# Zero rows, later reciprocals, a fourth step masked on VectorE, and early expert units in an attention and expert kernel

## The chip, the cores and the metric

The kernel runs on one core of one Trainium2 chip. The metric is the device time of one execution in microseconds, as the median of several runs. A profiled execution gives the trace; its span goes from the first to the last instruction.

## The reference

Three parts follow one another. All arithmetic is float32.

```python
# attention: q, k, v of (2, 8, 576, 64); each row of scores keeps its 32 largest
scores = scale * q @ k^T
kth = np.partition(scores, -32, axis=-1)[..., -32:-31]
scores = np.where(scores >= kth, scores, -1e9)
attn = exp(scores - max); attn = attn / (sum(attn) + 1e-09)
x = attn @ v                                   # put together as (1152, 512)
# experts: 4 of them, w1 (4, 512, 1024), w2 (4, 1024, 512)
p = domain_probs / (domain_probs.sum(-1) + 1e-09)
x = sum_e p[:, e] * (relu(x @ w1[e]) @ w2[e])
# gated layer: w_a, w_b (512, 1536), w_out (1536, 512), given in float64
out = ((x @ w_a) * (x @ w_b)) @ w_out
```

## The kernel before, in words

**Tokens.** The 576 positions of a batch are 4 tiles of 128 rows and a remainder of 64 rows (`REM`); the two remainders make a ninth tile, `MIX`. The nine tiles stand in four groups of 1, 2, 3 and 3 tiles. Attention goes by *steps*: for each group, for each of four pairs of heads, one step for each tile, 36 in all (steps 0 to 3, 4 to 11, 12 to 23, 24 to 35). A step has two heads, x = 0 and 1.

**One step.** TensorE makes the scores, ScalarE copies them out of PSUM (line 582), VectorE finds the 32 largest by four rounds of MAX8 (line 603) and three MATCH_REPLACE8 (609) for each head. Then a chain: GpSimd makes the two end values (649), ScalarE a steep ReLU (656), GpSimd the difference (659), ScalarE the exponential with its sum (666), GpSimd adds 1e-9 (675), VectorE takes the reciprocal (676), ScalarE scales the rows (679). TensorE transposes them (line 365), ScalarE copies the transposes out (706 for the 512 full columns, 710 for the last 64), and TensorE multiplies by v (362): for each head four products over 128 rows and one over 64 rows, the two heads side by side in 64 columns each. Step 3 (`URGENT`) ends the first group; there the difference and the addition run on VectorE. At the last tile of a pair the columns are copied out: into `xf` for the first group (738), into `xs` as a high and a low part for the others (744, 746).

**Experts and gated layer.** The first group's tile runs in float32 (`plain`): w1 and w2 are loaded as they are into places `wraw` (3) and `pw` (1) of 512 KB each, every fourth load into `pw`. The first of its eight halves of the first layer is done pair by pair, as the pairs' columns come. The other groups (`experts`) run on weights split into two float32r parts: a raw place, then ScalarE (767), then GpSimd or VectorE (768) into one of four split places. An expert's first layer needs the columns of all four pairs of its group. After all groups the gated layer runs, with its own split of the float64 weights.

**Order.** Nothing is in the order of the code. Each operation is added to a `Plan` with an engine, a duration, a key and the places it uses; `Plan.order` walks through time with these durations, takes on each engine the ready operation with the lowest key, and gives places out as they come free. The result is the order of issue on each engine, and each engine keeps it on the chip. Attention has keys by its step number, expert work 500 and 1000 upwards, evictions and weight differences negative ones, which go first. All loads go out on one queue, SyncE's.

Of the kernel before, what the change touches and what calls it, by code (L numbers as in the profile page):

```python
# [16 lines left out]
TOPK = 32  # L17
# [17 lines left out]
class Slots:  # L35


    def __init__(self, name, aps, region=None, spans=None):
        self.name, self.aps, self.region, self.spans = name, aps, region, spans
        self.free = set(range(len(aps)))  # L40
        self.queue, self.next = [], 0

# [33 lines left out]
class Plan:  # L76
# [14 lines left out]
    def order(self):  # L91
# [72 lines left out]
        while len(done) < len(self.ops):  # L164
# [32 lines left out]
            while queue and queue[0][0] <= now:  # L197
                _, _, op = heapq.heappop(queue)
                if op is None:
                    continue  # L200
                for t in op.tiles:
                    t.users -= 1
                    if not t.users:
                        t.slots.free.add(t.slot)
# [33 lines left out]
PAIRED, URGENT = (), 3  # L238


def body(tc, q, k, v, probs, w1, w2, wa, wb, wo, out):
# [42 lines left out]
    ident = const("ident", [128, 128])  # L284
    identr = const("identr", [128, 128], F32R)
    pr = const("pr", [128, NT, E])
# [5 lines left out]
    vrem = [const(f"vrem{b}", [REM, H, D]) for b in range(B)]  # L292
# [14 lines left out]
    raw = Region("raw", 3 * 1024, F32)  # L307
    wraws = raw.slots("wraw", 3, 1024)
    low = Region("low", 12800, F32)
# [27 lines left out]

    ps = psp.tile([128, 8, 512], F32, name="ps", tag="ps")
# [45 lines left out]
    def consts():  # L384
        make_identity(nc, ident)
        nc.vector.tensor_copy(identr, ident)
        nc.gpsimd.memset(qm.bitcast(F32), 0.0)
        nc.gpsimd.memset(facs[:, :, 0], -scale)
        nc.gpsimd.memset(facs[:, :, 1], STEEP)

    ready = gpsimd(1900, consts, -1e6, (), ())

    loads = []
    for i, t in enumerate(TILES):
        for rows_, view in token_rows(t, probs):
            loads.append(load(lambda i=i, rows_=rows_: pr[rows_, i], lambda view=view: view, 2.0, nbytes=4096))
# [7 lines left out]
    shared = vector(900, shares, 3.5, loads, ())  # L404
# [13 lines left out]
    def keys(b, h2, key, eng):  # L418
# [27 lines left out]
        for j in range(2):  # L446
# [8 lines left out]
            o = tensor(5 * TURN_R, turn, key + 0.02, sp[j] + krem_done[b][h + j] + [ready], [at, st_])  # L455
# [21 lines left out]
    def start_pair(c, h2, n):  # L477
# [65 lines left out]
        for b in batches(tiles):  # L543
# [5 lines left out]
            if b not in vrem_done:  # L549
                vrem_done[b] = load(lambda b=b: vrem[b], lambda b=b: last_rows(v, b), n - 2.4, (), (), 131072)  # L550
        return pair

    def scores(pair, j, i, n):
# [24 lines left out]
        o = tensor(4 * len(bs) * mm_r(HALF), emit, n - AHEAD, after, [at] + used)  # L578
# [8 lines left out]
    def masked(sd, n):  # L587

        m8, ends, sums = m8s.tile(), endss.tile(), sumss.tile()
        W = TOPK + 17 if n in PAIRED else TOPK  # L590
        m8v = lambda: m8.ap[:, 0:2 * W].rearrange("p (x n) -> p x n", x=2)
# [3 lines left out]
        last = []  # L595

        def top(x, src, c0, rounds, width, key, done):

            for r in range(rounds):
# [5 lines left out]
                )  # L605
                if r < rounds - 1:
# [9 lines left out]
        for x in range(2):  # L616
            s = sd[x][0]
            key = n + (0.4 if urgent else 0.001) * x
            if n not in PAIRED:
                last.append(top(x, [lambda s=s: s.ap, lambda x=x: e[x].ap], 0, TOPK // 8, S, key, sd[x][1]))  # L620
                continue


            got = []
            for i, op in enumerate((ALU.max, ALU.min)):
                half = lambda x=x, i=i: e[x].ap[:, i * HALF:(i + 1) * HALF]
                po = gpsimd(
                    pool_(HALF), lambda s=s, half=half, op=op: nc.gpsimd.scalar_tensor_tensor(half(), s.ap[:, 0:HALF], 1.0, s.ap[:, HALF:S], op0=ALU.mult, op1=op),
                    n - 0.4 + 0.1 * i, [sd[x][1]], [s, e[x]],
                )  # L630
                got.append(top(x, [half, half], TOPK * i, TOPK // 8 // (i + 1), HALF, key + 0.005 * i, po))

            o = vector(
                85, lambda x=x: nc.vector.tensor_tensor(
                    m8v()[:, x, TOPK:TOPK + 16], m8v()[:, x, TOPK - 2:TOPK - 18:-1], m8v()[:, x, TOPK:TOPK + 16], op=ALU.min
                ), -600, got, [m8],
            )
            last.append(vector(
                85, lambda x=x: nc.vector.tensor_reduce(
                    out=m8v()[:, x, TOPK + 16:W], in_=m8v()[:, x, TOPK - 1:TOPK + 16], axis=mybir.AxisListType.X, op=ALU.max  # L640
                ), -600, [o], [m8],
            ))

        ks = -3000 if urgent else n + 0.1
        out_, ex = [], []
        for xs_ in ([0], [1]) if urgent else ([0, 1],):
            x0, x1 = xs_[0], xs_[-1] + 1
            en = gpsimd(
                150, lambda x0=x0, x1=x1: nc.gpsimd.tensor_tensor(endv()[:, x0:x1], m8v()[:, x0:x1, ::W - 1], facs[:, x0:x1], op=ALU.mult),  # L649
                -4000 if urgent else -500, [last[x] for x in xs_] + [ready], [m8, ends],  # L650
            )
            for x in xs_:
                s = sd[x][0]

                a = scalar(
                    S, lambda x=x, s=s: nc.scalar.activation(e[x].ap, s.ap, AF.Relu, bias=endv()[:, x, 1:2], scale=-STEEP),  # L656
                    ks, [en], [s, e[x], ends], sbuf=True, ptr=True,
                )
                sub = lambda eng, x=x, s=s: eng.tensor_tensor(e[x].ap, s.ap, e[x].ap, op=ALU.subtract)  # L659
                if urgent:  # L660
                    b = vector(dve(S), lambda sub=sub: sub(nc.vector), ks, [a], [s, e[x]], port=True)
                else:
                    b = gpsimd(pool_(S), lambda sub=sub: sub(nc.gpsimd), ks, [a], [s, e[x]])
                ex.append(scalar(
                    S,
                    lambda x=x: nc.scalar.activation(  # L666
                        e[x].ap, e[x].ap, AF.Exp, bias=endv()[:, x, 0:1], scale=scale, accum_out=sums.ap[:, x:x + 1]
                    ),
                    ks, [b], [e[x], ends, sums], sbuf=True, ptr=True, extra=92,
                ))  # L670
            sv = lambda x0=x0, x1=x1: sums.ap[:, x0:x1]
            if urgent:
                sm = vector(70, lambda sv=sv: nc.vector.tensor_scalar(sv(), sv(), 1e-9, None, op0=ALU.add), ks, ex[-1:], [sums])
            else:
                sm = gpsimd(290, lambda sv=sv: nc.gpsimd.tensor_scalar(sv(), sv(), 1e-9, None, op0=ALU.add), -500, ex, [sums])
            rc = vector(70, lambda sv=sv: nc.vector.reciprocal(sv(), sv()), ks if urgent else -500, [sm], [sums])  # L676
            for x in xs_:
                out_.append((e[x], scalar(
                    S, lambda x=x: nc.scalar.activation(e[x].ap, e[x].ap, AF.Copy, scale=sums.ap[:, x:x + 1]),  # L679
                    ks, [rc], [e[x], sums], sbuf=True, ptr=True,  # L680
                )))
# [4 lines left out]
    def weigh(pair, i, ed, n):  # L686
# [6 lines left out]
        for e, done in ed:  # L693
# [8 lines left out]
            o = tensor(4 * TURN_F + 40, turn, n + 0.5, [done, ready], [at, e])  # L702
# [379 lines left out]
```

## Time and profile before

| what | us |
|---|---|
| median of 3 runs (lowest, highest) | 867.97 (867.55, 869.35) |
| the profiled execution's own time | 866.53 |
| its span | 864.7 |
| TensorE busy | 826.5 |
| VectorE busy | 715.8 |
| ScalarE busy | 544.6 |
| GpSimd busy | 265.2 |

TensorE is granted 0.998 of its clock on average. Busy times overlap one another; an engine's idle time is the span less its busy time, and what it costs depends on the stage in which it lies.

### The profile page before, as it was taken

To read this page: it belongs to the slowest core of one execution; us is meant where nothing else is said; L and a number is where in the kernel's file an instruction comes from. 1 tells how busy PE (TensorE), PEld (TensorE's weight loads), DVE (VectorE), ACT (ScalarE), POOL (GpSimd) and SP (SyncE) were. 2 spreads that over 40 slices of the span, in tenths; PEclk is the share of its full clock that TensorE was granted. 3 is DMA by queue.
4 is the path that set the end of the run, shared out by engine and by line. 5 is a ranking of instruction groups with operands and counts; after the bars stand their busy time and mean duration, and the time that the engine had idled before them with its cause. 6 is when DMAs were issued, how large, how long until landed. Compare 5 with 4: busy or idle time off the path is not lost. (4 is left out here: it accounts for less than half of the span.)

```text
span 864.7 us, 14129 instructions
## 1 busy us (share of the span) xinstructions
PE 826.5 (96%) x5168; PEld 728.0 (84%) x5168; DVE 715.8 (83%) x1381; ACT 544.6 (63%) x1042; POOL 265.2 (31%) x245
## 2 busy tenths in 40 slices
PE   5579999999999999999999999999999999999997
PEld 4466777788888888889888888889999989999996
DVE  6899999999999999999978999555434888999723
ACT  5888987899989998877765655333324535344310
POOL 2634442887897965853320000000000000000000
PEclk9999999999999999999999999999999999999999
DMA  7727977844564444342234556434101313323003
GB/s 197 244 90 257 297 239 235 268 149 145 168 185 150 152 148 153 98 123 97 75 122 156 179 177 195 122 122 128 44 1 49 98 49 98 91 81 98 25 1 109
DMA packets 83509, 117.06 MB, mean 135 GB/s; under 512 B 10608, under 2 KB 54640, under 8 KB 83440
## 3 DMA queue, kind: packets, MB, share of 16 engines
q1 hardware_dynamic: 83440, 116.17, 42.9%
q8 instruction: 40, 0.66, 0.3%
q14 instruction: 29, 0.24, 0.1%
HBM read 109.07 MB, written 7.08 MB: 134 GB/s over the span
## 5 line engine op out<-in xcount | busy, mean ns | idle before, releaser
L603 DVE MAX8 low<-low 128x8 f32<-128x576 f32 x288 | 203.7, 747 | 3.4 <-ACT low L582 3.3
L362 PE MATMUL ps<-xs,mid 128*128 128x384 f32 (+1 forms) x1152 | 205.1, 322 | 1.3 <-POOL mid L768 1.0
L362 PE MATMUL ps<-mid 128*128 128x512 f32 x768 | 198.6, 396 | 2.1 <-DVE mid L841 2.0
L362 PEld LDWEIGHTS ps<-xs,mid 128*128 128x128 f32 x1152 | 184.4, 189 | 11.5 <-issue 2.5
L362 PEld LDWEIGHTS ps<-mid 128*128 128x128 f32 x768 | 139.2, 188 | 28.5 <-DVE mid L841 6.0
L609 DVE MATCH_REPLACE8 low<-low 128x576 f32<-128x576 f32 x216 | 159.3, 743 | 0.0
L362 PE MATMUL ps<-xs,big 128*128 128x384 f32 x864 | 152.8, 335 | 0.0
L362 PEld LDWEIGHTS ps<-xs,big 128*128 128x128 f32 x864 | 149.9, 188 | 1.6 <-DVE low L1033 0.3
L767 ACT ACTIVATE mid<-raw 128x1024 fp32r<-128x1024 f32 x96 | 101.5, 1059 | 66.3 <-issue 39.9
L768 POOL TENSOR_TENSOR mid<-raw,mid 128x1024 fp32r<-128x1024 f32 x48 | 115.2, 2408 | 11.9 <-ACT mid L767 8.9
L659 POOL TENSOR_TENSOR low<-low 128x576 f32<-128x576 f32 x70 | 98.9, 1428 | 32.8 <-ACT low L656 31.0
L362 PE MATMUL ps<-big,mid 128*128 128x512 f32 x324 | 75.1, 390 | 0.0
L768 DVE TENSOR_TENSOR mid<-raw,mid 128x1024 fp32r<-128x1024 f32 x48 | 58.5, 1220 | 18.9 <-ACT mid L767 18.7
L362 PEld LDWEIGHTS ps<-big,mid 128*128 128x128 f32 x324 | 60.7, 188 | 12.3
L837 ACT ACTIVATE mid<-ps 128x384 fp32r<-128x384 f32 (+1 forms) x96 | 42.7, 450 | 33.0 <-PE ps L362 28.3
L859 DVE SCALAR_TENSOR_TENSOR ys<-ps,pr,ys 128x512 f32<-128x512 f32 x56 | 41.5, 747 | 24.3 <-PE ps L362 23.7
L841 DVE SCALAR_TENSOR_TENSOR mid<-ps,mid 128x384 fp32r<-128x384 f32 (+1 forms) x96 | 48.0, 506 | 15.1 <-ACT mid L837 14.6
L656 ACT ACTIVATE low<-low 128x576 f32<-128x576 f32 x72 | 53.4, 772 | 7.6 <-POOL low L649 7.4
L1012 ACT ACTIVATE low<-ps 128x384 f32<-128x384 f32 x36 | 17.6, 489 | 64.1 <-PE ps L362 64.0
L365 PE MATMUL ps<-ident,low 128*128 128x128 f32 (+1 forms) x360 | 50.6, 282 | 7.3 <-ACT low L679 7.1
L679 ACT ACTIVATE low<-low 128x576 f32<-128x576 f32 x72 | 52.9, 776 | 6.1 <-DVE low L676 6.1
L666 ACT ACTIVATE low<-low 128x576 f32<-128x576 f32 x72 | 55.7, 774 | 0.7 <-POOL low L659 0.7
(76 smaller groups left out, 1040.0 us busy)
## 6 DMA issues: line engine op xcount, KB each, us to landing
raw<-in_moe_w_dram SPq DMA_DIRECT2D x120, 512.0 KB, 3.7
big<-kscr SPq DMA_DIRECT2D x20, 576.0 KB, 4.8
low<-in_v_dram SPq DMA_DIRECT2D x24, 256.0 KB, 4.1
low<-in_moe_w_a_dram SPq DMA_DIRECT2D x12, 512.0 KB, 3.8
low<-in_moe_w_b_dram SPq DMA_DIRECT2D x12, 512.0 KB, 3.8
low<-in_moe_w_out_dram SPq DMA_DIRECT2D x12, 512.0 KB, 3.6
kscr<-big SPq DMA_DIRECT2D x8, 576.0 KB, 4.4
ys<-in_moe_w_dram SPq DMA_DIRECT2D x8, 512.0 KB, 4.6
```

What stands on the lines that cost most here:

```text
L362: nc.tensor.matmul(out, l, r, **kw)
L365: nc.tensor.transpose(out, a, i)
L603: 62 + 1.04 * width, lambda at=at, cs=cs: nc.vector.max(m8v()[:, x, cs], at()), key + 0.02 * r, [done],
L609: lambda at=at, cs=cs: nc.vector.match_replace(out=src[1](), in_to_replace=m8v()[:, x, cs], in_values=at(), imm_value=LOW),
L656: S, lambda x=x, s=s: nc.scalar.activation(e[x].ap, s.ap, AF.Relu, bias=endv()[:, x, 1:2], scale=-STEEP),
L659: sub = lambda eng, x=x, s=s: eng.tensor_tensor(e[x].ap, s.ap, e[x].ap, op=ALU.subtract)
L666: lambda x=x: nc.scalar.activation(e[x].ap, e[x].ap, AF.Exp, bias=endv()[:, x, 0:1], scale=scale, accum_out=sums.ap[:, x:x + 1]),
L679: S, lambda x=x: nc.scalar.activation(e[x].ap, e[x].ap, AF.Copy, scale=sums.ap[:, x:x + 1]),
L767: hi = scalar(1024, lambda: nc.scalar.activation(u.ap[:, 0:1024], r.ap, AF.Copy), 500 + s, [ld], [u, r], sbuf=True)
L768: sub = lambda eng: eng.tensor_tensor(u.ap[:, 1024:2048], r.ap, u.ap[:, 0:1024], op=ALU.subtract)
L837: n, lambda h=h, p=p: nc.scalar.activation(h.ap[:, 0:n], p.ap[:, 0:n], AF.Relu), -1000, [o], [h, p]
L841: lambda h=h, p=p: nc.vector.scalar_tensor_tensor(h.ap[:, n:2 * n], p.ap[:, 0:n], 0.0, h.ap[:, 0:n], op0=ALU.max, op1=ALU.subtract),
```

## The change

- **Zero rows.** `vrem`, the v rows of the remainder, becomes 128 rows high, and the transposed places `pt` get zeros in rows 64 to 127 of their last block, once. The value product of the remainder then runs over 128 rows like the others.
- **Later reciprocals.** GpSimd's addition of 1e-9 is planned 1200 ns longer (`SLACK`), so that the order has VectorE's reciprocal later.
- **The fourth step** goes through `hurried`: the exponential is taken of all scores as soon as the first round has given the maximum; after the last round VectorE masks and sums in one instruction, adds, takes the reciprocal and scales. ScalarE's ReLU and scaling and the differences fall away there.
- **Fourth weight place.** `wraw` has 4 places, taken from the region `low` and from `ident`, which becomes a view of `identr`.
- **Early units and banks.** Three halves of the first group's first layer (two of expert 0, one of expert 1) are done pair by pair, in three PSUM banks at once; their w1 comes in row slabs of 512 and 256 KB, every fifth load into `pw`.
- **Ahead.** The first four weight units of the second group are queued before the last expert of the first group.
- **Rest.** In the plan a loaded place comes free 1200 ns after its last use. The loads of the probabilities and their normalization get later keys, and several durations of the plan are new.

An unused branch (`PAIRED`) is removed as well.

```diff
@@ Plan.order
-                    if not t.users:
+                    if not t.users and t.slots.rest:
+                        heapq.heappush(queue, (now + t.slots.rest, -2 - op.n - 0.1 * op.tiles.index(t), t))
+                    elif not t.users:
                         t.slots.free.add(t.slot)
@@ body
-    vrem = [const(f"vrem{b}", [REM, H, D]) for b in range(B)]
+    vrem = [const(f"vrem{b}", [128, H, D]) for b in range(B)]
...
-    wraws = raw.slots("wraw", 3, 1024)
+    wraws = raw.slots("wraw", 4, 1024)
...
+    for s in (kspls, bts, kraws, vts, qraws, wraws, pws):
+        s.rest = REST
...
+    def zeros():
+        for b in range(B):
+            nc.gpsimd.memset(vrem[b][REM:128], 0.0)
+        for p in pts.aps:
+            nc.gpsimd.memset(p[REM:128, MAIN:MAIN + 128], 0.0)
+    zeroed = gpsimd(1500, zeros, 0.2, [ready], ())
...
-            loads.append(load(... pr[rows_, i] ..., 2.0, nbytes=4096))
+            loads.append(load(... pr[rows_, i] ..., 4.0, nbytes=4096))
...
-    shared = vector(900, shares, 3.5, loads, ())
+    shared = vector(900, shares, 5.2, loads, ())
...
-            o = tensor(5 * TURN_R, turn, key + 0.02, sp[j] + krem_done[b][h + j] + [ready], [at, st_])
+            o = tensor(640, turn, key + 0.02, sp[j] + krem_done[b][h + j] + [ready], [at, st_])
@@ masked
+        if urgent:
+            return hurried(sd, n, m8v, m8, ends, endv, sums, firsts, last)
...
         sm = gpsimd(290, lambda: nc.gpsimd.tensor_scalar(sums.ap, sums.ap, 1e-9, None, op0=ALU.add), -500, ex, [sums])
+        sm.lag += SLACK
         rc = vector(70, lambda: nc.vector.reciprocal(sums.ap, sums.ap), -500, [sm], [sums])
...
+    def hurried(sd, n, m8v, m8, ends, endv, sums, firsts, last):
+        for x in range(2):
+            s, e = sd[x][0], es.tile(n)
+            en = gpsimd(150, ... endv()[:, x, 0:1] = m8v()[:, x, 0:1] * facs ..., -4000, [firsts[x], ready], [m8, ends])
+            ex = scalar(S, ... activation(e.ap, s.ap, AF.Exp, bias=endv()[:, x, 0:1], scale=scale), n + 0.1, [en], ...)
+            def mask(x=x, s=s, e=e, sv=sv):
+                nc.vector.scalar_tensor_tensor(
+                    e.ap, s.ap, m8v()[:, x, TOPK - 1:TOPK], e.ap, op0=ALU.is_ge, op1=ALU.mult, accum_out=sv()
+                )
+                nc.vector.tensor_scalar(sv(), sv(), 1e-9, None, op0=ALU.add)
+                nc.vector.reciprocal(sv(), sv())
+                nc.vector.tensor_scalar(e.ap, e.ap, sv(), None, op0=ALU.mult)
+            out_.append((e, vector(1450, mask, -3000, [ex, last[x]], [s, e, m8, sums], port=True)))
@@ weigh
-                        l, rows = (vt[:, j, m], 128) if m < M4 else (vrem[b][:, pair.h + j], REM)
+                        l = vt[:, j, m] if m < M4 else vrem[b][:, pair.h + j]
...
-                            ov()[j * D:(j + 1) * D, i, r0:r1], l, pt[j].ap[0:rows, m * 128 + r0:m * 128 + r1],
+                            ov()[j * D:(j + 1) * D, i, r0:r1], l, pt[j].ap[:, m * 128 + r0:m * 128 + r1],
...
-            1150, emit, n + 0.6, ptd + ...
+            1245, emit, n + 0.6, [zeroed] + ptd + ...
@@ experts
-                    unit = w_unit(w1[e, :, u:u + 256].rearrange("(a p) n -> p a n", p=128), KD, late)
+                    unit = ahead.pop(u) if u in ahead else w_unit(w1[e, :, u:u + 256].rearrange("(a p) n -> p a n", p=128), KD, late)
@@ plain
+        early = [(0, 0), (0, 512), (1, 0)]
+        banks = {k: ms.tile() for k in early}
+        done = {}
+        for a in range(KD):
+            for e, w in ((0, 1024), (1, 512)):
+                r, rd, rv = plain_unit(w1[e, a * 128:(a + 1) * 128, 0:w].rearrange("(a p) n -> p a n", p=128), 1, w)
+                for f0 in range(0, w, 512):
...
+                    done[e, f0] = tensor(4 * mm_f(128), emit, 1000 + nxt(), [done.get((e, f0))] + rd + xdone[c, a], [p, r])
...
+                if e == E - 1:
+                    for u in range(f0, f0 + 512, 256):
+                        ahead[u] = w_unit(w1[0, :, u:u + 256].rearrange("(a p) n -> p a n", p=128), KD, 0)
```

## Rows read from the trace of the kernel before

**Rows 1.** Windows by stage: length, busy us of each engine (instructions), clock, DMA.

```profile
37.00:67.00 30.00, 21.50 (x177) 17.14 (x174) 28.68 (x67) 25.96 (x58) 12.20 (x18) 0.94 0.33 99
67.00:153.00 86.00, 83.88 (x627) 64.84 (x626) 82.05 (x177) 71.33 (x144) 34.85 (x41) 1.00 0.80 259
...
163.00:305.00 142.00, 138.78 (x1058) 122.12 (x1057) 139.06 (x302) 127.75 (x253) 121.40 (x89) 1.00 0.53 162
305.00:457.00 152.00, 150.36 (x1083) 133.17 (x1081) 138.74 (x274) 119.42 (x240) 75.37 (x68) 1.00 0.37 119
```

**Rows 2.** Timeline of VectorE and of TensorE, 303 to 307: start, us, instruction, count.

```profile
304.78 0.56 DVE L746 TENSOR_TENSOR xs<-ps,xs 128x384 fp32r<-128x384 f32 x1
...
306.52 0.69 PE L362 MATMUL ps<-xs,mid 128*128 128x384 f32 x3
```

**Rows 3.** Timeline of VectorE at 281 and GpSimd from 283 and 138.

```profile
280.81 2.73 DVE L603 MAX8 low<-low 128x8 f32<-128x576 f32 x4
...
283.92 4.77 POOL L768 TENSOR_TENSOR mid<-raw,mid 128x1024 fp32r<-128x1024 f32 x2
288.63 1.43 POOL L659 TENSOR_TENSOR low<-low 128x576 f32<-128x576 f32 x1
290.01 2.43 POOL L768 TENSOR_TENSOR mid<-raw,mid 128x1024 fp32r<-128x1024 f32 x1
...
140.64 2.80 POOL L659 TENSOR_TENSOR low<-low 128x576 f32<-128x576 f32 x2 [1.16 <-ACT low L656]
```

**Rows 4.** TensorE: groups by form, then timeline from 100 and 333.

```profile
L362 PE MATMUL ps<-low 128*64 128x128 f32 x512 | 35.0, 279 | 0.0
...
100.87 1.09 PE L362 MATMUL ps<-low 128*64 128x128 f32 x16
101.89 0.44 PE L362 MATMUL ps<-low,vrem 64*64 64x128 f32 x4
102.26 0.79 PE L362 MATMUL ps<-big 128*128 128x288 f32 x4
...
104.11 1.05 PE L362 MATMUL ps<-xf,raw 128*128 128x128 f32 x8
...
333.64 0.69 PE L362 MATMUL ps<-low 128*64 128x64 f32 x16
...
335.39 1.33 PE L362 MATMUL ps<-big,qm 128*128 128x288 f32 x8
```

**Rows 5.** Timeline of GpSimd at the start; in brackets the idle time before.

```profile
1.23 0.95 POOL L387 MEMSET qm<- 128x1024 f32 x1
...
12.39 2.10 POOL L413 TENSOR_TENSOR big<-low,big 128x512 fp32r<-128x512 f32 x3 [10.13 <-ACT big L409]
```

**Rows 6.** Groups of VectorE by line, 8 to 283: busy us, mean ns, idle before.

```profile
L841 DVE SCALAR_TENSOR_TENSOR mid<-ps,mid 128x256 fp32r<-128x256 f32 x27 | 10.9, 413 | 0.9 <-ACT mid L837 0.9
L859 DVE SCALAR_TENSOR_TENSOR ys<-ps,pr,ys 128x512 f32<-128x512 f32 x10 | 7.5, 748 | 1.4 <-PE ps L362 1.3
L676 DVE RECIPROCAL low<-low 128x2 f32<-128x2 f32 (+1 forms) x23 | 3.6, 157 | 5.1 <-POOL low L675 5.1
...
L659 DVE TENSOR_TENSOR low<-low 128x576 f32<-128x576 f32 x2 | 1.4, 748 | 0.0
```

**Rows 7.** One line of VectorE, the gated layer's maximum: duration ns min/median/max.

```profile
L971 DVE TENSOR_SCALAR low<-low x36: 415/420/430, 456.9 to 806.2; 128x512 f32<-128x512 f32 x36
```

**Rows 8.** Timeline of the fourth step's end, 48 to 70.

```profile
51.89 1.41 DVE L603 MAX8 low<-low 128x8 f32<-128x576 f32 x2
...
58.85 1.44 ACT L679 ACTIVATE low<-low 128x576 f32<-128x576 f32 x2
...
66.01 0.28 ACT L738 ACTIVATE xf<-ps 128x128 f32<-128x128 f32 x1 [1.82 <-PE ps L362]
```

**Rows 9.** Timeline at the start of step 1.

```profile
18.97 0.65 ACT L582 ACTIVATE low<-ps 128x576 f32<-128x576 f32 x1
...
19.41 1.40 DVE L603 MAX8 low<-low 128x8 f32<-128x576 f32 x2
```

More of the change, by code (lines that the diff above doesn't have):

```diff
@@ L644, in masked @@
[L644 to L681, printed above, removed]
@@ new lines, in masked @@
+            last.append(top(x, [lambda s=s: s.ap, lambda x=x: e[x].ap], 0, TOPK // 8, S, key, sd[x][1]))
+        if urgent:
+            return hurried(sd, n, m8v, m8, ends, endv, sums, firsts, last)
+        ks = n + 0.1
+        out_, ex = [], []
+        en = gpsimd(
+            150, lambda: nc.gpsimd.tensor_tensor(endv(), m8v()[:, :, ::TOPK - 1], facs, op=ALU.mult), -500, last + [ready], [m8, ends]
+        )
+        for x in range(2):
+            s = sd[x][0]
+            a = scalar(
+                S, lambda x=x, s=s: nc.scalar.activation(e[x].ap, s.ap, AF.Relu, bias=endv()[:, x, 1:2], scale=-STEEP),
+                ks, [en], [s, e[x], ends], sbuf=True, ptr=True,
+            )
+            b = gpsimd(
+                pool_(S), lambda x=x, s=s: nc.gpsimd.tensor_tensor(e[x].ap, s.ap, e[x].ap, op=ALU.subtract), ks, [a], [s, e[x]]
+            )
+            ex.append(scalar(
+                S,
+                lambda x=x: nc.scalar.activation(
+                    e[x].ap, e[x].ap, AF.Exp, bias=endv()[:, x, 0:1], scale=scale, accum_out=sums.ap[:, x:x + 1]
+                ),
+                ks, [b], [e[x], ends, sums], sbuf=True, ptr=True, extra=92,
+            ))
@@ new lines, in masked @@
+        sm = gpsimd(290, lambda: nc.gpsimd.tensor_scalar(sums.ap, sums.ap, 1e-9, None, op0=ALU.add), -500, ex, [sums])
+        sm.lag += SLACK
+        rc = vector(70, lambda: nc.vector.reciprocal(sums.ap, sums.ap), -500, [sm], [sums])
+        for x in range(2):
+            out_.append((e[x], scalar(
+                S, lambda x=x: nc.scalar.activation(e[x].ap, e[x].ap, AF.Copy, scale=sums.ap[:, x:x + 1]),
+                ks, [rc], [e[x], sums], sbuf=True, ptr=True,
+            )))
+        return out_
@@ L731, in weigh @@
         pair.od.append(tensor(
-            1150, emit, n + 0.6, ptd + sum((pair.vd[b] for b in bs), []) + [vrem_done[b] for b in bs], [pair.o] + pt + [pair.v[b] for b in bs]
+            1245, emit, n + 0.6, [zeroed] + ptd + sum((pair.vd[b] for b in bs), []) + [vrem_done[b] for b in bs], [pair.o] + pt + [pair.v[b] for b in bs]
         ))
@@ L893, in plain, with emit @@
         yd = {}
+        early = [(0, 0), (0, 512), (1, 0)]
[5 more added lines that the diff above has]
+                for f0 in range(0, w, 512):
+                    p = banks[e, f0]
+                    def emit(a=a, f0=f0, rv=rv, p=p):
+                        for s in range(4):
+                            mm(
+                                p.ap[:, s * 128:(s + 1) * 128], rv()[:, 0, f0 + s * 128:f0 + (s + 1) * 128], xf[:, a],
+                                start=(a == 0 and s == 0), stop=(a == KD - 1 and s == 3),
+                            )
+                    done[e, f0] = tensor(4 * mm_f(128), emit, 1000 + nxt(), [done.get((e, f0))] + rd + xdone[c, a], [p, r])
         for e in range(E):
@@ L896, in plain @@
             for f0 in range(0, F, 512):
-                p = ms.tile()
+                if e == E - 1:
+                    for u in range(f0, f0 + 512, 256):
+                        ahead[u] = w_unit(w1[0, :, u:u + 256].rearrange("(a p) n -> p a n", p=128), KD, 0)
+                p = banks[e, f0] if (e, f0) in early else ms.tile()
                 p2 = p2 if f0 else ms.tile()
                 h = hfs.tile()
-                last = None
-                us = []
-                for u in range(0, 512, 256):
+                last = done.get((e, f0))
+                for u in range(0, 512, 256) if (e, f0) not in early else ():
                     r, rd, rv = plain_unit(w1[e, :, f0 + u:f0 + u + 256].rearrange("(a p) n -> p a n", p=128), KD)
-                    us.append((r, rd, rv))
-                    if e == 0 and f0 == 0:
-                        continue
                     for i in range(2):
```

84 lines of the change are left out of this document (37 added, 47 removed).

## The prediction, as it was put on record

> **What bounds the kernel now.** I read the busy times by stage first [rows 1]. TensorE idles 8.5 us between 37 and 67, 2.1 between 67 and 153, 3.2 between 163 and 305, 1.6 between 305 and 457. So a large gain can come only from TensorE work that goes away or from the early idle time. But TensorE is not alone: between 37 and 305 VectorE is as full (28.68 of 30, 82.05 of 86, 139.06 of 142), because it runs the top-32 rounds of one step after another. The reader is to see two full engines, and to ask which of them sets the next milestone.
>
> The milestones are the ends of the four attention groups, since the expert work of a group needs all its columns. The third (steps 12 to 23) shows the balance [rows 2]: VectorE writes its last columns at 304.78, done at 305.34, and TensorE starts the new group at 306.52. TensorE had almost nothing left of the group before when the data came. Ahead of that point an earlier TensorE alone gains little: it would wait for VectorE's milestone. Behind it TensorE is the bound: 150.36 of 152 us up to 457, with VectorE at 138.74 [rows 1]; what is won at 305 stays won, and less TensorE work counts in full.
>
> How long the milestone lags VectorE is the next view [rows 3]. The last maxima of step 23 end near 282.2 (the four that start at 280.81 end at 283.54 with those of step 24). Its first difference on GpSimd starts at 288.63, behind two weight differences (283.92, 4.77), and its second waits for one more (290.01, 2.43). In step 11 the same two run back to back at 140.64. So some 22 us pass from maxima to columns here, with queues on GpSimd in them.
>
> **The change, part by part.**
>
> *Zero rows.* A normal value product is 16 records of 128 rows, then 4 of 64 rows [rows 4]: starts at 100.87, 101.89 and, of what comes next, 102.26. The 16 records are 1.09 us, the last one 0.28 as their mean is, so their 15 intervals take 0.81, 54 ns each; the step to the 64-row form then takes 1.02 - 0.81 = 0.21, and the last four take 3 x 0.054 and another 0.21. With one shape for all 20: 19 x 0.054 + 0.21 = 1.24 for 1.39, 0.15 saved. A mixed unit has two groups with half the columns, 333.64 to 335.39, 1.75; half of 54 ns is 27, I take 30, so 40 records in one shape take 39 x 0.030 + 0.21 = 1.38, 0.37 saved. Units behind 305 (steps 24 to 35): 8 x 0.15 + 4 x 0.37 = **2.7 us**. The 24 before it give 3.6, which only the milestone can cash. Bounds: 0, if the end of each unit costs more, to 2.7. The zeros themselves are five GpSimd memsets; one of 1024 words takes 0.95, and these have 512 or 128, so they are under 4 together, in the 10.13 us that GpSimd idles until 12.39 [rows 5]; without that cover the second key split would be later by as much. The Trainium skill, TensorEngine Tiling (Array Packing), Performance Considerations, says the opposite of this edit: a contraction of 64 rows should use row tiling, for up to twice the speed. By it the padded part would take double; here the 64-row records step by 54 ns like the full ones [rows 4], so the trace doesn't agree.
>
> *Later reciprocals.* In 8 to 283 us VectorE waits 5.1 us for GpSimd's sums ahead of a reciprocal [rows 6], 23 of them. The planner now places them 1.2 us later, so that top-k instructions stand in front. I take all **5.1** for VectorE (bounds 2 to 5.1). What is late next: the normalizing copies; the chain of step 23 gets one top-k instruction longer, **0.75** by the top-k rows around it (0 to 1.5).
>
> *Fourth step on VectorE.* Per head, a difference of 0.75 [rows 6] becomes a masked product, which I price the same, and a scaling is added: 0.42 for 512 elements [rows 7], 0.47 for 576. Two heads cost VectorE **0.94**; the sum that comes with the mask could add 0 to 0.16 each (a small instruction such as the reciprocal, [rows 6]), I take 0. For the chain it is a cut: from the last maxima (51.89 + 1.41 = 53.3) to the last scaled row (58.85 + 1.44 = 60.3) 7.0 us pass [rows 8], now about 3 for both heads. With the transposes ready on time, the columns of 66.01 could come up to 9 us earlier.
>
> *Early units and three banks.* When a pair's columns come, TensorE now runs 24 records instead of 8 (104.11, 1.05 us [rows 4]; less 0.28 that is 0.11 from start to start): 16 more, 1.8, four times. Three of the four fall into the 8.5 us of idle time, 5.4. The two added loads are small; all slabs together are 3 MB, and DMA has a share of 0.33 between 37 and 67 [rows 1]. TensorE's lead at 305 is then at most about 5.4 here, 3 of the remaining idle time, and 3.6 by zero rows: **12**. Price if the slabs go out ahead of the keys of steps 1 to 3: step 1's scores are copied at 18.97 and VectorE turns to step 1 at 19.41 [rows 9], no slack, so up to some 6 us of VectorE's gain could go again. Ten small probability loads leave SyncE's early queue, which makes room; I take 0.
>
> *Fourth weight place, rest, first units of the next group ahead of the last expert, new durations.* No instruction is added. Loads are planned 1.2 us later, and the fourth place covers it: in the stage of 305 to 457 DMA has a share of 0.37. The units ahead hold all four split places, so that second-layer units wait for one; attention work fills that. I take 0 (bounds -1 to +2).
>
> **The sum.** Milestone of 305: VectorE 5.1 - 0.94 = 4.2 earlier, less 0.75 for the chain, 3.4. TensorE's lead of some 10 us draws evictions ahead of the top-k: 10.9 + 7.5 us of them up to 283 [rows 6], 0.15 of the 120 us since 163, so 1.5 back: 1.9. Of the weight differences that stood ahead of and between those of step 23 (4.77 and 2.43) I take 2.0 away, bounds 0 to 7.2, near the lower end since GpSimd stays full, 121.40 of 142. TensorE's own leftover between 305.34 and 306.52 will be done: 1.0. Together 4.9, under the lead of 12. Behind it 2.7. 7.6 in all, of which I leave 0.3 for new short waits: **7.3**. The profiled span of 864.7 becomes 857.4; its own time was 866.53, 1.83 more, so 859.2; the median of the runs shown lies 1.44 above that one: **860.7 us**.
>
> **Rivals.**
> - *The lead is kept whole.* GpSimd has split the weights by 280, step 23's chain is as short as step 11's, and the lead of 12 is cashed: 12 + 2.7 = 14.7, 853.3. For: the two queued differences. Against: VectorE idles only 2.9 us between 163 and 305 and has no more to give.
> - *Only the products behind 305 count.* The milestone stays: slabs ahead of keys eat the 5.1, or the later reciprocals and queues do. 868.0 - 2.7 = 865.3. For: no slack in step 1. Against: VectorE's wait is real time in which its next input lay ready.
> - *Slower: GpSimd's queue at step 23.* With TensorE ahead, the four split places of the next experts are filled at 4 x 2.4 = 9.6 us just when the maxima of step 23 end, weights standing ahead of differences in the planner. They replace the 2.43 to 7.2 that stand there now: 304.8 - 1.9 + 9.6 less these, 305.3 to 310.1, with TensorE idle until then: up to 5 later, less 2.7. It decides from some 5 us of added queue on (1.9 for the milestone, 2.7 for the products); at the most 870.
> - *The zero rows don't do what they are for.* If a record of 128 rows took twice one of 64, each unit would pay 4 x 0.054 more and give -0.07 for 0.15: the 2.7 falls to about -1, 864.4. Against: the step of 54 ns in both forms. It is the rule of the Trainium skill's page named above that would have it so.
>
> **How the numbers follow.** Forecast 0.43 (its own range 857 to 864), lead kept 0.2, products alone 0.2, slower 0.13, row tiling 0.04. 0.2% (1.7 us) is about what a measurement of this kernel can tell. Faster: 0.43 + 0.2 + 0.04 and 0.17 of the products alone (the rest, 0.03, lies within 0.2%): 0.84. Of the slower case 0.05 lies within, 0.08 above: same 0.08, slower 0.08. The range from 854 to 867.5 leaves out half of the kept lead, 0.1, and 0.08 above.
>
> **What would show it.** After: value products as 20 records of one shape in 1.24 us; no 64-row value product; reciprocal waits under 1.5 us; the fourth pair's columns before 60; the first experts' start near 150 to 153; the third group's near 300 to 302, with TensorE idle ahead of it and VectorE full; the idle of 37 to 67 down to about 3. Wrong would be: VectorE idle in steps 1 to 3 for scores, the third group starting at 305 or later, or products with the same 1.39.

## The result and the profile after

The changed kernel takes **860.69 us** (median of 4 runs, 860.27 to 862.2) beside 867.96 us before (4 runs, 867.55 to 869.35) on the same chip: ratio 0.9917, 95% interval 0.9899 to 0.9934. The forecast was 860.7. The number came out; the mechanism that the forecast put behind most of it did not, and that is what the experiments are about. The span is 858.5 us, 6.2 less than before; TensorE's mean granted clock is 0.993, before 0.998.

The windows by stage, after, answer to [rows 1]; the columns are the same (length, busy us of PE, PEld, DVE, ACT, POOL, then granted clock, DMA share, GB/s):

```profile
0.00:37.00 37.00, 21.12 (x95) 17.36 (x96) 29.11 (x62) 25.33 (x54) 16.80 (x31) 1.00 0.77 241
37.00:67.00 30.00, 24.56 (x217) 21.96 (x217) 28.74 (x66) 23.60 (x53) 10.73 (x16) 0.94 0.46 149
67.00:153.00 86.00, 82.17 (x606) 63.23 (x603) 85.90 (x187) 75.47 (x153) 45.80 (x46) 0.98 0.81 268
153.00:305.00 152.00, 150.72 (x1166) 133.09 (x1165) 150.84 (x330) 139.93 (x288) 120.21 (x95) 1.00 0.53 168
305.00:457.00 152.00, 149.94 (x1059) 134.60 (x1058) 142.18 (x278) 118.69 (x230) 71.72 (x62) 0.99 0.37 118
```

Two windows of before that [rows 1] doesn't hold are needed beside them:

```profile
0.00:37.00 37.00, 22.58 (x114) 18.89 (x114) 27.17 (x58) 25.58 (x56) 14.04 (x25) 1.00 0.81 240
153.00:305.00 152.00, 148.56 (x1117) 129.31 (x1116) 148.82 (x323) 137.75 (x272) 128.73 (x96) 1.00 0.55 171
```

Read TensorE's idle time, length less the first busy figure. Between 37 and 67 it falls from 8.50 to 5.44. But it grows from 14.42 to 15.88 ahead of 37 and from 2.12 to 3.83 up to 153: over the first 153 us it is 25.0 before and 25.1 after. **The early idle time was moved, not saved.** From 153 to 305 it falls from 3.44 to 1.28, and behind 457 by another 1.3; over the whole span the idle time goes from 38.2 to 35.2 (span less the busy total of the page). Then read the clock: it is below 1.00 in three windows now, in one before.

The value products are as forecast. TensorE's timeline around 303 and 328, after, beside [rows 4]:

```profile
303.23 1.09 PE L375 MATMUL ps<-low 128*64 128x128 f32 x16
304.15 0.39 PE L375 MATMUL ps<-low,vrem 128*64 128x128 f32 x4
304.47 0.97 PE L375 MATMUL ps<-mid 128*128 128x512 f32 x3
305.27 0.68 PE L375 MATMUL ps<-xs,mid 128*128 128x384 f32 x3
...
328.00 0.69 PE L375 MATMUL ps<-low 128*64 128x64 f32 x16
328.52 0.29 PE L375 MATMUL ps<-low,vrem 128*64 128x64 f32 x4
328.63 0.64 PE L375 MATMUL ps<-low 128*64 128x64 f32 x16
329.10 0.29 PE L375 MATMUL ps<-low,vrem 128*64 128x64 f32 x4
329.32 1.33 PE L375 MATMUL ps<-big,qm 128*128 128x288 f32 x8
```

A unit takes 304.47 - 303.23 = 1.24 for 1.39 before, a mixed one 329.32 - 328.00 = 1.32 for 1.75. There is no 64-row value product left. With 0.15 for each of 32 units and 0.43 for each of 4, TensorE's work is 6.5 us shorter.

Now the milestone. The third group's last columns, which ended at 305.34 before [rows 2], are written here:

```profile
294.51 0.54 DVE L767 TENSOR_TENSOR xs<-ps,xs 128x384 fp32r<-128x384 f32 x1
```

They end at 295.05, 10.3 us earlier. Yet the group's first expert product starts at 305.27 (the fourth row of the timeline above), 1.25 us earlier than at 306.52 [rows 2], and nothing stands in brackets behind it: TensorE did not wait for it, it had other work. Before it was the same: TensorE is busy without a gap from 300.00 to 306.52. The gated layer's first product, which waits for all groups, starts 6.4 earlier (625.93; 632.36 before).

VectorE really did get ahead. Groups of its instructions by line between 8 and 283, after, beside [rows 6]:

```profile
L881 DVE SCALAR_TENSOR_TENSOR ys<-ps,pr,ys 128x512 f32<-128x512 f32 x10 | 7.4, 741 | 0.1
L671 DVE RECIPROCAL low<-low 128x2 f32<-128x2 f32 x22 | 3.3, 152 | 2.0 <-POOL low L668 2.0
```

Its waits for sums fell from 5.1 to 2.0, and its waits for TensorE in the evictions from 1.4 to 0.1. Step 23's last maxima end at 273.6 instead of 282.2. TensorE was not waiting for them.

The fourth step's end, in the timeline of all engines, beside [rows 8]:

```profile
50.03 0.21 POOL L668 TENSOR_SCALAR low<-low 128x2 f32<-128x2 f32 x1 [0.68 <-ACT low L663]
...
50.95 0.82 DVE L695 SCALAR_TENSOR_TENSOR low<-low 128x576 f32<-128x576 f32 x1 [0.15 <-ACT low L689]
51.70 0.08 DVE L695 DVE_READ_ACCUMULATOR low<-low 128x1 f32 x1
51.81 0.15 DVE L698 TENSOR_SCALAR low<-low 128x1 f32<-128x1 f32 x1
52.00 0.16 DVE L699 RECIPROCAL low<-low 128x1 f32<-128x1 f32 x1
52.20 0.52 DVE L700 TENSOR_SCALAR low<-low 128x576 f32<-128x576 f32 x1
...
54.32 0.16 DVE L671 RECIPROCAL low<-low 128x2 f32<-128x2 f32 x1
...
55.40 2.39 PE L378 MATMUL ps<-identr,low 128*128 128x128 f32 x10 [3.75 <-ACT low L674]
...
68.19 0.28 ACT L759 ACTIVATE xf<-ps 128x128 f32<-128x128 f32 x1 [0.58 <-PE ps L375]
```

Both heads' masks and scalings run from 50.95 until step 2's reciprocal starts at 54.32, 3.4 us. They hold this reciprocal back: its sum on GpSimd (first line) was done at 50.24, so it stands 4.1 us late, its copies behind it, and TensorE idles 3.75 us for step 2's rows. The fourth pair's columns come at 68.19, later than the 66.01 of before.

Last, the clock. One window of the changed kernel (columns as above; 0.50 is 1.2 GHz, 1.00 is 2.4 GHz), TensorE's timeline in it, and the same products at the full clock, in the kernel of experiment 6 below:

```profile
136.80:140.20 3.40, 3.40 (x16) 3.33 (x17) 3.40 (x8) 3.14 (x7) 1.48 (x2) 0.50 0.99 302
```

```profile
136.73 2.36 PE L378 MATMUL ps<-identr,low 128*128 128x128 f32 x10 [1.93 <-ACT low L674]
138.74 1.96 PE L375 MATMUL ps<-big 128*128 128x288 f32 x8
...
144.75 1.98 PE L375 MATMUL ps<-raw,low 128*128 128x512 f32 x4 [0.82 <-ACT low L954]
```

```profile
135.27 1.43 PE L378 MATMUL ps<-identr,low 128*128 128x128 f32 x10 [0.76 <-ACT low L674]
138.06 1.44 PE L375 MATMUL ps<-big 128*128 128x288 f32 x8 [1.37 <-ACT low L727]
...
143.89 1.98 PE L375 MATMUL ps<-raw,low 128*128 128x512 f32 x4 [1.16 <-ACT low L954]
```

TensorE is counted as full at 136.80, but the ten transposes take 2.36 us for 1.43 and the eight score products 1.96 for 1.44. There are three such stretches of 3.4 us (at 54.9, 136.8 and 317.7), beside idle gaps of 3.75, 1.93 and 1.50 + 0.56 us; before there was one, at 42.7. By such pairs of the same instructions, an estimate, the three make TensorE 1.2, 1.45 and 1.33 us longer busy, 4.0 together (the last on 21 products of 384 columns, 5.40 us for 4.07 in experiment 2's kernel), and that of before 1.2.

So TensorE's time divides like this: idle time -3.0, products -6.5, half clock +2.8, together -6.7, for 6.2 that the span fell; 0.5 stays open. This is an account of two executions and not of causes: a half clock can stand in for a wait. The rows above show it: from the ten transposes to the products of 512 columns, 8.02 us pass after and 8.62 in experiment 6's kernel at the full clock, where TensorE waits for ScalarE instead.

### The profile page after: what moved, and what is told of

Same layout as the page of the kernel before. It is cut to its first block, busy times and chain, and to the rows that moved or that the text cites. A ratio compares the mean times of both kernels' runs of the same rounds, so it can differ in the third digit from the quotient of the medians.

```text
span 858.5 us, 14179 instructions
## 1 busy us (share of the span) xinstructions
PE 823.3 (96%) x5168; PEld 730.5 (85%) x5168; DVE 715.5 (83%) x1385; ACT 540.4 (63%) x1036; POOL 265.3 (31%) x250
## 4 chain that ended last, share of the span: by engine, by line
PE 76%; DVE 15%; ACT 3%; DMA 2%; issue 1%; POOL 1%; SPq 1%; DVEq 0%; ACTq 0%; POOLq 0%
PE ps L375 70%; DVE low L624 6%; PE ps L378 5%; DVE low L632 5%; DVE mid L789 1%; DMA low<-in_q_dram 1%; SPq L359 1%; DVE mid L863 1%; DVE ys L881 1%; DMA qrem<-in_q_dram 1%; ACT low L674 1%; POOL low L659 0%; DMA low<-in_k_dram 0%; ACT low L663 0%; ACT mid L788 0%
## 5 line engine op out<-in xcount | busy, mean ns | idle before, releaser
L375 PEld LDWEIGHTS ps<-xs,mid 128*128 128x128 f32 x1152 | 186.7, 190 | 10.5 <-issue 1.3
L674 ACT ACTIVATE low<-low 128x576 f32<-128x576 f32 x70 | 51.3, 774 | 14.1 <-DVE low L671 14.1
L378 PE MATMUL ps<-identr,low 128*128 128x128 f32 (+1 forms) x360 | 50.7, 286 | 6.5 <-ACT low L674 6.1
L655 ACT ACTIVATE low<-low 128x576 f32<-128x576 f32 x70 | 52.5, 776 | 5.9 <-POOL low L649 5.6
L663 ACT ACTIVATE low<-low 128x576 f32<-128x576 f32 x70 | 54.5, 778 | 1.4 <-POOL low L659 1.4
```

What stands on the lines that cost most here:

```text
L375: nc.tensor.matmul(out, l, r, **kw)
L378: nc.tensor.transpose(out, a, i)
L663: lambda x=x: nc.scalar.activation(e[x].ap, e[x].ap, AF.Exp, bias=endv()[:, x, 0:1], scale=scale, accum_out=sums.ap[:, x:x + 1]),
```

## The experiments

The theory on record: up to 305 VectorE's milestone sets the time, behind it TensorE. The rival that the profile after suggests: TensorE's whole work sets the time from 67 on, and VectorE has slack. The expectations call the rival T, and the theory on record M or V. Each ratio is to the kernel before, run in turn on the same chip; there were five rounds for each. The experiments ran on four chips, with medians of the kernel before from 867.1 to 868.6, so the ratios compare better than the times.

**1. Zero rows alone, and only up to step 23.** Both are the kernel before with its order kept; the diff is the second's, the first has `high = 128` throughout. The places `pt` get their zeros as in the change.

```diff
-    vrem = [const(f"vrem{b}", [REM, H, D]) for b in range(B)]
+    vrem = [const(f"vrem{b}", [128, H, D]) for b in range(B)]
...
+            high = 128 if n < 24 else REM
-                        l, rows = (vt[:, j, m], 128) if m < M4 else (vrem[b][:, pair.h + j], REM)
+                        l, rows = (vt[:, j, m], 128) if m < M4 else (vrem[b][0:high, pair.h + j], high)
```

> The kernel before with the zero rows alone, in the unchanged order of issue. Theory T (TensorE sets the end in every stage behind 67 us, so each us of its work counts in full): 24 early units at 0.15, 8 late normal ones at 0.15, 4 mixed ones at 0.37, 6.3 us less than before. Rival M (as predicted: VectorE's milestone near 305 us bounds the time, products ahead of it are free): 2.7 us less.

> The kernel before with zero rows used in the products of steps 0 to 23 alone; steps 24 to 35 keep 64 rows. T: 3.6 us less than before. M: no change to 1 us less.

Measured: 864.02 us, ratio 0.9955 (0.9943 to 0.9968), and 865.90 us, 0.9982 (0.9973 to 0.9991). Both lie between what T and M give. Between the two runs lie the units behind 305: 0.0027 of 868, 2.3 us (uncertain by some 1.3), against the 2.7 of the forecast. The units ahead of 305, which by the theory only the milestone could cash, are worth 1.6 alone; by the interval 0.8 to 2.3, so M's upper end of 1 us is not excluded, while T's 3.6 is. TensorE's timeline of the second kernel, one of its windows, and the same 21 products in the kernel before:

```profile
167.57 0.53 PE L365 MATMUL ps<-ident,ys 128*128 128x128 f32 x2 [1.25 <-DVE mid L846]
168.83 0.47 PE L365 MATMUL ps<-ident,ys 128*128 128x128 f32 x1 [0.73 <-DVE mid L846]
169.03 4.10 PE L362 MATMUL ps<-xs,mid 128*128 128x256 f32 x21
...
168.70:172.10 3.40, 3.27 (x15) 3.26 (x16) 3.38 (x9) 0.91 (x3) 3.32 (x4) 0.50 0.85 254
```

```profile
170.27 2.98 PE L362 MATMUL ps<-xs,mid 128*128 128x256 f32 x21
```

Here a stretch at 1.2 GHz, which costs these products 1.1 us, stands behind two short gaps. The kernel before has gaps of 1.10 and 0.73 at the same place, and 1.00 of the clock. Whether that is what is missing from the 3.6 is not shown: executions of this kernel at a mean clock of 0.989 took 865.8 to 866.3 us, those at 0.995 took 865.1 to 867.1.

**2. The changed kernel without zero rows**, its order kept: the remainder's product over 64 rows again.

```diff
-                        l = vt[:, j, m] if m < M4 else vrem[b][:, pair.h + j]
+                        l, rows = (vt[:, j, m], 128) if m < M4 else (vrem[b][0:REM, pair.h + j], REM)
```

> The changed kernel with its remainder products over 64 rows again, in the same order of issue. T: 6.3 us more than the changed kernel, so near 867. M: 2.7 us more, near 863.4.

Measured: 864.96 us, 0.9970 (0.9959 to 0.9982), again between T and M. On top of the other parts zero rows are worth 4.3 us (4.6 by the ratios), all other parts together 2.6 (0.0030 of 868). The two add up: 0.9955 x 0.9970 = 0.9925, the change 0.9917.

This kernel also has the gaps that stand beside the change's third half-clock stretch, here in TensorE's timeline:

```profile
320.45 0.44 PE L378 MATMUL ps<-identr,ys 128*128 128x128 f32 x2 [1.51 <-DVE mid L863]
321.44 0.44 PE L378 MATMUL ps<-identr,ys 128*128 128x128 f32 x2 [0.55 <-DVE xs L905]
```

Its granted clock stays at 1.00 there. So gaps of this size do not suffice for a half clock.

**3. Less work for VectorE.** The changed kernel, in which step 5, or step 14, leaves out 8 VectorE instructions (some 5.5 us); the order is the same. That step then keeps 16 scores for a row instead of 32. Its last two MAX8 rounds go in the same way as the replacements in the diff, and its second round writes to the place of the last.

```diff
-                        lambda at=at, cs=cs: nc.vector.match_replace(
+                        lambda at=at, cs=cs, r=r: n == 5 and r > 0 or nc.vector.match_replace(
```

> The changed kernel without VectorE's last two maxima and the two replacements ahead of them in step 5 (it keeps 16 scores a row there); nothing else in the order of issue changes. 8 instructions, some 5.5 us of VectorE near 70 us. Theory V (VectorE sets the pace up to the third group's start): 4 to 5.5 us less than the changed kernel, 855.5 to 857. Theory T (TensorE sets it behind 67 us): under 1 us less.

> The same in step 14, near 162 us, so inside the stage of 153 to 305. V: 4 to 5.5 us less than the changed kernel. T: under 1 us.

Measured: 860.62 us, 0.9920 (0.9907 to 0.9933), and 860.12 us, 0.9916 (0.9903 to 0.9929): nothing that these runs can tell, as T has it; the intervals leave up to some 2 us. The window of the first shows where the work went:

```profile
67.00:153.00 86.00, 82.30 (x607) 63.08 (x606) 79.93 (x175) 76.05 (x154) 45.82 (x46) 0.98 0.82 270
```

VectorE is 79.93 busy instead of 85.90, six microseconds of idle time in a stage in which it was full, and TensorE is busy for 82.3 us as in the change (82.17). A full engine was not a bound.

**4. More work for TensorE.** The same kernel with the value products of steps 5 to 9, or 14 to 18, made twice (the result is the same), some 5.4 us.

```diff
-            for r0, r1, b in groups:
+            for r0, r1, b in groups * (2 if n in (5, 6, 7, 8, 9) else 1):
```

> The changed kernel with the value products of steps 5 to 9 made twice (the second time over the first, same result): 5 x 1.08 = 5.4 us more of TensorE between 85 and 135 us. V: 0 to 1.5 us more than the changed kernel. T: 5.4 us more, 866.

> The same in steps 14 to 18, between 185 and 235 us. V: 0 to 1.5 us more than the changed kernel. T: 5.4 us more, 866.

Measured: 865.09 us, 0.9963 (0.9948 to 0.9978), and 864.29 us, 0.9965 (0.9953 to 0.9978): 4.4 and 3.6 us of the 5.4 are paid (4.0 and 4.2 by the ratios). With experiment 3 this decides for the rival in the changed kernel: between 85 and 235 us TensorE's work counts at 0.7 to 0.8, and VectorE's at nothing that shows. The kernel before had no such run: VectorE's work was not taken away there.

**5. Step 2's reciprocal moved ahead of the fourth step's masks**, nothing else in the order changed (`soon` holds each step's sum and reciprocal).

```diff
+    for n, sm, rc in soon:
+        if n == URGENT - 1:
+            rc.start = min(rc.start, sm.start + 390)
+    for op in sorted(ops, key=lambda o: (o.start, o.n)):
```

> The changed kernel with one instruction moved: the reciprocal of step 2 stands ahead of the two masks of step 3 on VectorE and no longer behind them. T: TensorE's wait of 3.75 us at 55 us and the half clock after it (3.4 us, worth 1.7) go, VectorE waits up to 0.9; 3 to 5 us less than the changed kernel, 856 to 858. M: under 1 us, since VectorE's work ahead of the milestone stays the same.

Measured: 860.66 us, 0.9922 (0.9908 to 0.9935), no gain: T's 856 to 858 were missed, and M's bound of 1 us holds. TensorE's waits between 37 and 153 (us, times, longest), first after, then this kernel:

```profile
PE ps L378 <- ACT low L674: 6.1, 3, 3.7
PE ps L375 <- ACT low L954: 1.9, 3, 0.8
PE ps L375 <- ACT xf L759: 0.9, 2, 0.5
```

```profile
PE ps L378 <- ACT low L674: 3.0, 3, 1.9
PE ps L375 <- ACT xf L759: 2.8, 3, 1.9
PE ps L375 <- ACT low L954: 2.2, 3, 1.2
```

The gap of 3.75 is gone, and the next waits grow: 8.9 us in these rows of the change, 8.0 in this kernel's, and the end does not move. A wait taken away this early shows up again a few steps later; that too little TensorE work is ready here is a reading of these rows, not a test.

**6. All reciprocals early again.** As in 5, with the condition left out.

> The changed kernel with the later reciprocals undone alone: each reciprocal stands on VectorE where the addition of GpSimd is planned to end, all else keeps its place. V (as predicted, VectorE's waits for the sums count): its 5.1 us come back, 3 to 5 us more than the changed kernel, 864 to 866. T (TensorE sets the end): VectorE's waits are free, TensorE's waits at 55 us (3.75) and 136.7 us (1.93) with the half clock behind each go or move as in the run with one reciprocal moved; 0 to 4 us less, 857 to 861.

Measured: 860.27 us, 0.9905 (0.9891 to 0.9919), the same as the change, as T has it. But VectorE's waits for sums, between 8 and 283, are 2.7 us here for 2.0 in the change:

```profile
L671 DVE RECIPROCAL low<-low 128x2 f32<-128x2 f32 x22 | 3.9, 178 | 2.7 <-POOL low L668 2.6
```

In this order the later reciprocals save VectorE 0.7, not 5.1, so the run does not price the largest term of the forecast; that VectorE's time counts for nothing here rests on experiment 3. Of the change's three half-clock stretches only the last is left, and the time is still the same.

**7. One early bank**, and the order planned anew: one half of the first layer goes pair by pair, as before the change, and 512 columns of w1 come in slabs.

```diff
-        early = [(0, 0), (0, 512), (1, 0)]
+        early = [(0, 0)]
...
-            for e, w in ((0, 1024), (1, 512)):
+            for e, w in ((0, 512),):
```

> The changed kernel with one early half and bank instead of three; the order is planned anew. T: TensorE's work of 16 records at each of four pairs, 7.2 us, moves out of the idle time between 37 and 67 us; 3 to 5 us more than the changed kernel, 864 to 866. V (as predicted, the lead of 12 us is far more than VectorE's milestone can cash): no change to 1 us more.

Measured: **858.23 us**, 0.9886 (0.9869 to 0.9903), the lowest of all, 2.5 below the change (2.7 by the ratios, whose intervals overlap by 0.0004). Both T and V had expected it no faster. Its windows:

```profile
37.00:67.00 30.00, 23.14 (x198) 19.32 (x197) 27.99 (x65) 24.78 (x54) 10.66 (x16) 0.94 0.49 150
67.00:153.00 86.00, 82.83 (x621) 64.08 (x622) 85.68 (x187) 74.29 (x152) 42.21 (x45) 1.00 0.80 259
...
305.00:457.00 152.00, 151.85 (x1101) 137.01 (x1100) 143.01 (x282) 119.73 (x236) 72.75 (x64) 1.00 0.35 112
```

More idle time up to 67 (6.86 for 5.44), less behind it (3.17 for 3.83, then 0.15 for 2.06). Over the span TensorE idles as long as in the change (35.3 us) and is busy 2.3 less: the half-clock stretches at 136.8 and 317.7 are not there. Step 23's maxima end at 278.2, 4.6 later than in the change, and the kernel is faster: once more not VectorE's milestone. As the order is another one, this doesn't price the banks by themselves.

**8. One early bank with all reciprocals early** (7 and 6 together, 7's order otherwise).

> The kernel with one early bank, its planned order kept on every engine, except that VectorE's reciprocals of all steps stand where GpSimd's sum is planned to end, and not 1.2 us later. Theory (TensorE is the bound behind 67 us, VectorE's waits for sums cost nothing): the same as the kernel with one early bank, 857.5 to 859.5 us. Rival (the later reciprocals serve only where one bank leaves VectorE ahead, and the waits of some 3 to 5 us come back into the sum): 861 to 863 us. Rival (an earlier chain lets TensorE's remaining early idle time of 6.9 us between 37 and 67 shrink, since step 2's reciprocal no longer stands behind step 3's masks): 855 to 857 us.

Measured: 860.2 us, 0.9921 (0.9907 to 0.9935), between what the theory and its first rival give. So with one bank the later reciprocals are worth 2 us, or 3 by the ratios. VectorE's waits for sums between 8 and 283, in experiment 7's kernel and then in this one:

```profile
L671 DVE RECIPROCAL low<-low 128x2 f32<-128x2 f32 x22 | 3.6, 165 | 2.6 <-POOL low L668 2.6
```

```profile
L671 DVE RECIPROCAL low<-low 128x2 f32<-128x2 f32 x22 | 3.3, 152 | 4.9 <-POOL low L668 4.8
```

Here 2.3 us of them did come back, and the time rose by about as much. TensorE idles 1.0 more between 67 and 153 (4.12) and 0.7 over the span. So in this order VectorE's waits may count after all; these runs leave it open.

**9. The fourth step's end as before**, the order planned anew: ReLU and exponential with its sum on ScalarE, the difference on VectorE, a scaling on ScalarE.

```diff
-            ex = scalar(S, ... activation(e.ap, s.ap, AF.Exp, bias=endv()[:, x, 0:1], scale=scale), n + 0.1, [en], ...)
...
-            out_.append((e, vector(1450, mask, -3000, [ex, last[x]], [s, e, m8, sums], port=True)))
+            a = scalar(S, ... AF.Relu, bias=endv()[:, x, 1:2], scale=-STEEP ..., [en], ...)
+            b = vector(dve(S), ... tensor_tensor(e[x].ap, s.ap, e[x].ap, op=ALU.subtract), ..., [a], ...)
+            ex = scalar(S, ... AF.Exp, ... accum_out=sums.ap[:, x:x + 1] ..., [b], ...)
```

> The changed kernel with the fourth step's end as before (ReLU and scaling on ScalarE, difference on VectorE); the order is planned anew. T: the columns of the fourth pair came at 68.2 us and not before 60, since the reciprocal of step 2 stood behind the masks, so the masks gained nothing: within 2 us of the changed kernel. V: VectorE's 0.94 us come back, 1 us less.

Measured: 873.63 us, 1.0052 (1.0037 to 1.0066), 13 us slower than the change and slower than before, where T had it within 2 us and V 1 us less. The cost is not where the edit is. Its window and TensorE's waits, 153 to 305:

```profile
153.00:305.00 152.00, 144.56 (x1106) 128.44 (x1105) 147.44 (x319) 132.51 (x274) 112.85 (x92) 0.98 0.51 162
```

```profile
PE ps L378 <- ACT low L674: 2.8, 1, 2.8
PE ps L375 <- DVE mid L869: 2.1, 1, 2.1
PE ps L378 <- DVE mid L869: 2.0, 1, 2.0
PE ps L375 <- POOL mid L795: 0.6, 1, 0.6
```

TensorE idles 7.4 us there for 1.3 in the change, and its granted clock falls to 0.50 in six stretches over the span instead of three. Over the span it idles 9.3 us more. The edit's own step ends near 70 us; the cost is put down to the order that the planner finds from another start, which no run separates from the edit. So this run doesn't price the fourth step's edit; it shows how much two planned orders can differ.

## Why the prediction was right, and where its steps were not

**What bounds the kernel, the step that failed.** "Ahead of that point an earlier TensorE alone gains little: it would wait for VectorE's milestone." It did not wait. The prediction named a sign of being wrong, "the third group starting at 305 or later", and it came: 305.27. [rows 2] showed TensorE starting the third group 1.2 us behind the columns, and the forecast took that for a handover with nothing left to do. It was TensorE working without a gap (6.52 us busy of the 6.52 ahead of the start), with attention work and leftover work of the second group that could stand on either side of the columns. With the columns 10.3 us earlier the group starts 1.25 earlier, and TensorE's idle time of 153 to 305 goes down, not up. Experiments 3 and 4 show it of the changed kernel. Of the kernel before it is shown in part only: products ahead of 305 pay there as well (experiment 1), by the medians at less than half of their work, and no run took VectorE's away. With one bank (experiment 8) it is open.

**Later reciprocals, 5.1 in the sum: 0.7 of VectorE, and nothing in the time.** VectorE's wait fell by 3.1 (to 2.0; "under 1.5" was forecast), but experiment 6 gives only 0.7 of that back: the rest of the fall isn't due to the place of the reciprocals alone, and the term was too large by itself. Step 23's maxima came 8.6 us earlier where the sum had 2.7 (4.2 less 1.5 for evictions). The 8.6 came from waits: up to step 23's last maxima VectorE is as busy as before (260.55 for 261.05 us) and idles 5.05 for 13.15. The terms of masks, chain, evictions and GpSimd's queue (0.94, 0.75, 1.5, 2.0) were sums on an engine that had slack where experiment 3 asked, whatever their sizes. For step 23 the lag from maxima to columns is 21.5 us now, 23.1 before.

**Products behind 305, 2.7: right.** 2.3 by experiment 1, uncertain by some 1.3; the work itself is 2.9. The interval of 1.24 is exact, the mixed one 1.32 for 1.38. The row tiling rival fell: a record over 128 rows steps no slower than one over 64 did, and of the 0.15 that a unit gains, 0.10 lies at the change of form inside it (0.92 us up to the first record of the remainder, 1.02 before) and 0.05 behind it. By the Trainium skill, TensorEngine Tiling (Array Packing), Performance Considerations, a contraction of 64 rows should gain by row tiling. Here filling it up with zeros to 128 rows gains 3.4 us of 867 by itself (experiment 1); no run lays two 64-row products side by side in row tiles, so the page's advice itself is not tested.

**Products ahead of 305, counted at nothing of their own:** 1.6 by experiment 1 (0.8 to 2.3), of 3.6 that they are; in the profiled execution a new half-clock stretch takes 1.1 of the rest.

**Early units, 5.4 of lead: nothing up to 153** (25.0 us of idle time before, 25.1 after), and the order with three banks is slower than that with one (experiment 7). The products fill idle time in 37 to 67, which fell to 5.44 ("about 3" was forecast); that they are then missing where they would have covered later waits is read from the windows of experiment 7, not shown by itself.

**Fourth step:** "about 3 for both heads" is 3.4. "Up to 9 us earlier" is 2.2 later. Its own figures, 7.0 less 3, gave 4 and not 9; and the step costed the masks and did not ask what is queued behind them. Step 2's reciprocal was, which the other part of the change had moved back. Undoing it (experiment 5) gains nothing.

**Why the number fitted all the same.** The sum had 7.6 from two sources, 4.9 of it through the milestone. The chip gave 6.5 of products and 3.0 of idle time, and took some of it back, 2.8 by the clock, which the sum didn't have at all. The forecast of the span was 7.3 less, and it came out 6.2 less; the median then lay 0.4 above the profiled execution, where 1.44 had been added for that. So the two misses of about 1 us cancelled. That the number is met to 0.1 us is chance. The third group "near 300 to 302 with TensorE idle ahead of it" and the first experts "near 150 to 153" (155.5, before 157.9) were the signs that could have told the mechanisms apart, and both were wrong.

**The rivals.** "Only the products behind 305 count" had slabs in the way of the keys; steps 1 to 3 end their maxima at 30.5, 40.1 and 50.8, 1.7 to 3.0 earlier than before, so no key came late. "The lead is kept whole" needed TensorE to get ahead: its idle time up to 153 did not fall. The slower case by GpSimd's queue had no place to act, since TensorE did not wait for step 23's columns.

Open: the fourth weight place, the rest of loaded places and the units ahead were not run by themselves, and the 2.6 us of all parts but the zero rows are not divided among them. Open too: whether the half clock follows from the gaps ahead of it, or only often stands there (a gap of 2.44 us at 53.0 in experiment 7's kernel has none behind it, nor have those of 1.51 and 0.55 in experiment 2's), and which of the order's differences makes the kernel with one bank the fastest, and whether VectorE's waits count in it.

## What to carry to other kernels

Two engines can both be full for a hundred microseconds while only one of them is the bound. To tell which, look at what the second one's results wait for when they are early: if their consumer has other work that can be shifted, the second engine has slack, and its waits can be worth nothing. Take work away from one and add some to the other before any gain is priced on a handover.

Filling an odd last product up to the shape of its neighbours can be worth more than the rows that it wastes; read the interval from unit to unit, not the instructions' means. And where a planner makes the order, an edit's own cost is only part of what is measured: keep the order for one experiment, and plan anew for another.

## What the runs showed of the chip beyond that

- A full TensorE can be at half speed: at 136.80 its busy share is 100% at a granted clock of 0.50, and ten transposes take 2.36 us for 1.43. The busy share doesn't show it, the clock column does. An idle gap of 1.93 us stood ahead of it, in other kernels gaps of 1.25 and 0.73; but gaps of 1.51 and 0.55 stand in experiment 2's kernel at a clock of 1.00.
- An execution's mean clock doesn't give its time. The kernel of steps 5 to 9 (experiment 4) took 862.8 us at 0.998 and 864.7 to 865.7 at 0.994 to 0.995. The kernel before took 866.6 to 867.6 at 0.998 and 866.7 to 867.6 at 0.989 (the runs beside experiment 1).
- A masked product with its sum is an instruction of 0.82 us and one of 0.08 that reads the sum, together 0.15 above the 0.75 of the difference, near the upper end of what the forecast had left open (0 to 0.16). A scaling of 576 elements by a row's own factor takes 0.52, not the 0.47 worked out from 512.
